# RWKV-7 attention with a SoLU layer on one core: the output product as one run ahead of the transposes

## The chip, the cores and the metric

The program runs on one core of one Trainium2 chip. The metric is the device time of one execution in microseconds, from the runs of the whole kernel; lower is better. Before the change the median of three runs is 536.89 us (536.58, 536.89, 538.34).

## What is computed

Two blocks, all in fp32. First a recurrent attention over 4 batches, 8 heads, 768 positions and head size 40, then a feed-forward layer over the 3072 tokens that come out.

```
for t in range(S):                       # S = 768, state: D x D per batch and head
    y[:, :, t] = rt @ state
    Sa    = state @ at
    state = state * wt - outer(Sa, bt) + outer(vt, kt)

h    = x @ w_in                          # x: 3072 x 320, w_in: 320 x 1024
e    = exp(h - max(h));  solu = h * e / (sum(e) + 1e-9)
ln   = (solu - mean) / sqrt(var + 1e-6) * g_ln
out  = ln @ w_out                        # w_out: 1024 x 320
```

## The kernel before

The recurrence is computed in chunks of 64 positions. A chunk of two batches is one item of work; there are N = 24 items (2 pairs of batches, 12 chunks each), and items alternate between the two pairs of batches, each of which carries its own state. The kernel is a software pipeline written out by hand: every engine runs its instructions in the order in which the program issues them (`manual_schedule`). One turn of the main loop, for i from -1 to 26, is called a slot here. In slot i the kernel works on several items at once:

- item j = i + 5: the transposes of a (`front`) and b (`front_b`), the product of both (`norm`, tile py, result nt), and the start of the inverse of a small triangular matrix. The decay of item j + 2 is summed up (`decay_by_halves`, part of tile pst) and that of j + 1 transposed (`decay_turned`, ei to ex).
- item i + 1: the transposes of k and v (`attend_kv`, tile pkv, copied to kvT), of r (`attend_r`, tile pb, copied to rT) and of the state (`stated`, tile pst, copied to s); the scores (ps), the product of r and the state (psr), then px and the small products in py (`couple`, `close`).
- item i: the solve with the inverse (`solved`, tile pu, masked by VectorE and copied by ScalarE into lu), and the read-out (`read`, tile pyo; `summed` and `leave`, tiles tot, st and x).
- item c = i - 2: the first feed-forward product (`hidden`, tile h), the row maximum (nmax), exponential (e), weighing and spread (sq, var, rs).
- item c - 1: the transposes of e (`folded`, tile plnT, copied to lnT) and the second feed-forward product (`output`, tile po), which ScalarE scales into osb (`stored`) before SP's queue sends it out.

VectorE fills its time with steps of the inverse of two items together: lines 502 to 519, tiles prod and uu. The strings in `plans` say how many steps stand at which place; in slots from 6 on those of the even slots and those of the odd slots differ. In even slots four steps stand between bT and lu, in odd slots one, which is the first of a new inverse. Each step of this size consists of two products and two sums. GpSimd (POOL) scales b and k (line 393, tile kb), takes the power for rs and issues the stores of x and some other DMAs; SP issues most loads and the stores of the output.

PSUM is divided into four pairs of banks: A, B, C and h. A tile gets a pair by its tag, and a new tile with the same tag waits until all readers of the old one are done. From slot 5 on `turn` swaps B and C between the names X and Y in every slot, so that what was X in one slot is Y in the next. In the slots from 5 on, pair A holds in turn the transposes of a and b (pa), the state with the cumulative sums (pst), psr and pyo; X holds pb, ps, px; Y holds pkv, pu, py and po.

A detail that the change touches: from slot 5 to 22 the output product is cut in two (`FIRST = 6`, line 27 and line 1132). Six of its eight blocks of the inner dimension are multiplied at the end of the slot, the other two in the next slot after the transposes of a, b, k and v, followed by the scaling and the store. Each block is two matmuls of 160 columns in the program; the profile shows twice as many, so that a whole product is 32 and the parts are 24 and 8.

The block of the loop that the change edits is the `else` branch of a slot's first half (lines 1011 to 1040). Slot 5 (`i == EARLY - AHEAD`) is the first to run it; there the logarithm of the decay of item 7 (`logged`, tile lw) is issued inside the block. From slot 19 on there are no more items for the transposes of a and b.

Of the kernel before, what the change touches and what calls it, by code (L numbers as in the profile page):

```python
# [21 lines left out]
AHEAD = 5  # L22
LANDS_NEXT = {2: 6, 3: 7, 4: 8, 5: 11, 6: 9, 7: 10, 8: 12}
LAG = 2
EARLY = 10
NK = 5
FIRST = 6
SPLITS = {2: (0, 0, 0, 2, 4), 24: (0, 0, 0, 0, 2)}


# [23 lines left out]
def kernel(  # L54
# [24 lines left out]
    N = NPAIR * NCH  # L79
    NF = DFF // P  # L80
# [64 lines left out]
    def pair(tag, name):  # L145
        return psum.tile([P, 2, 512], FP32, tag=tag, name=name)

    turn = dict(X="B", Y="C")
# [165 lines left out]
    def ok(i):  # L314
        return 0 <= i < N
# [258 lines left out]
    def attend_kv(i, t):  # L574

        if not ok(i):
            return lambda: None
        d = st[i]
        for y, x in enumerate((d["kb"], v_t[0])):
            turned(t, y, x)  # L580
        o = two.tile([P, 2, 8, C], FP32, tag="kvT", name="kvT", bufs=1)
        d["kT"], d["vT"] = o[:, :, 0:4], o[:, :, 4:8]
        return lambda: nc.scalar.copy(out=o[0:W2].rearrange("p b j t -> p b (j t)"), in_=t[0:W2])

    def attend_r(i, t, y):
        if not ok(i):
            return lambda: None
        t = turned(t, y, r_t[0])

        def evict():  # L590
            st[i]["rT"] = kept("rT", t)
        return evict
# [73 lines left out]
    def solved(i):  # L666

        if not ok(i):
            return lambda: None
        d = st[i]  # L670
        t = pair(turn["Y"] if i >= LAG else "h", "pu")
        for u in in_turn(lambda p, q, g, h: (p ^ h, p)):
            p, q, g, h = u
            at, x = (2 * q + g) * W2, half(p ^ h)
            mm(t[half(p), h, at:at + W2], d["tu"][x, 4 * p + 2 * q + g, Q:], x0[x, h, 2 * q + g])
        lu = d["lu"] = two.tile([P, H, W2], FP32, tag="lu", name="lu", bufs=1)
        o, y = lu.rearrange("p (j h) c -> p h j c", h=2), t[:, :, 0:4 * W2].rearrange("p h (j d) -> p h j d", j=4)
        copy = lambda: nc.scalar.copy(out=o[:, :, :, C:], in_=y[:, :, :, C:])
        if i < LAG:
            copy()  # L680
            return lambda: masked(o[:, :, :, 0:C], y[:, :, :, 0:C])
        masked(o[:, :, :, 0:C], y[:, :, :, 0:C])
        return copy
# [159 lines left out]
    late, rest = [], []  # L843
# [129 lines left out]
    for i in range(-1, N + LAG + 1):  # L973
        j, c = i + AHEAD, i - LAG
        plan = plans.get(i, plans[N + i % GRP])
        if len(plan) > 6:
            plan, unflipped = plan[:2] + plan[3:], plan[2]
        else:
            unflipped = ""
        steady = i >= EARLY - AHEAD  # L980
        if i >= 0 and not steady:
            load_keys(j + 3, "w")
        if not steady:
            load_r(i + 3)
        elif i > EARLY - AHEAD and i % GRP:
            load_r(i + 2)
        if i == -1:
            load_values(2)
            land(4, nc.sync)
            land(len(lands), nc.sync)  # L990

        if i < EARLY - AHEAD:
            tc_, ta = pair("C", "pa"), pair("A", "pb")
            front_out, r_out = front(j, ta, 0), attend_r(i + 1, ta, 1)
            fold_out = folded(c - 1)
            ei_out, b_out = decay_turned(j + 1, tc_, 0), front_b(j, tc_, 1)
            kv_out = attend_kv(i + 1, pair(turn["X"], "pkv"))
            r_out()
            front_out()
            if i < EARLY - AHEAD:  # L1000
                vector(plan[0])
                fold_out()
                b_out()
            else:
                b_out()
                vector(plan[0])
                fold_out()
            s_out = stated(i + 1, pair("A", "pst"), 0) if ok(i + 1) else lambda: None
            for evict in (ei_out, kv_out, s_out):
                evict()  # L1010
        else:
            turn.update(zip("XY", ("BC", "CB")[(i - EARLY + AHEAD) % 2]))
            ta = pair("A", "pa")
            front_out, b_out = front(j, ta, 0), front_b(j, ta, 1)
            kv_out = attend_kv(i + 1, pair(turn["Y"], "pkv"))
            front_out()
            kv_out()
            b_out()
            if i == N + LAG:
                fold_out = folded(c - 1)  # L1020
            for products, stored in rest:
                products()
                if i == N + LAG:
                    late.append(stored)
                else:
                    stored()
            rest.clear()
            vector(plan[0])
            if i < N + LAG:
                fold_out = folded(c - 1)  # L1030
            ts = pair("A", "pst")
            s_out = stated(i + 1, ts, 0) if ok(i + 1) else lambda: None
            tc_ = pair(turn["X"], "pb")
            r_out, ei_out = attend_r(i + 1, tc_, 0), decay_turned(j + 1, tc_, 1)
            if i == EARLY - AHEAD and ok(j + 2):
                logged(j + 2)
            cum_out = decay_by_halves(j + 2, ts)
            for evict in (r_out, ei_out, fold_out, s_out, *late):
                evict()
            late.clear()  # L1040
        if not steady:
            left(i - 1)
        if i == EARLY - AHEAD:
            load_keys(j + 3, "w")

        early = i < EARLY - AHEAD or i > N - 2
        waves = (1, 0, 1, 0, 1, 0, 1, 1, 0, 0, 0) if early else (0, 0, 2, 1, 0, 0, 1, 1, 0, 0, 0)
        wave = iter(range(NK))

        def run(x):  # L1050
            for _ in range(waves[x]):
                hidden(c, next(wave))
            if sum(waves[:x + 1]) == NK and sum(waves[:x]) < NK:
                highest(c)

        run(0)
        if i >= EARLY - AHEAD:
            cum_out()
        solved(i)()
        vector(plan[1])  # L1060
        if not steady:
            load_keys(j + 2, "bak")
        run(1)
        scores(i + 1)()
        vector(unflipped)
        flip(i + 1)
        run(2)
        scaled(j + 1, "b")
        stated_r(i + 1)
        run(3)  # L1070
        norm(j)
        if ok(j) and j % GRP == GRP - 1:
            begin_inverse(j // GRP)
        scaled(j + 1, "k")
        by_value(i + 2)
        run(4)
        if i == LAG + 1:
            mean = mean_more(pair("A", "pmean")[:, 0], 6, NF, mean)
        carried(i + 1)
        run(5)  # L1080
        read(i, 0)
        if i >= 0:
            load_values(i + 3)
        if steady:
            left(i - 1)
            load_keys(j + 2, "ba" if i % GRP else "b")
            if i % GRP:
                load_r(i + 3)
        ahead = 2 + (i >= EARLY - AHEAD)
        if ok(j + ahead):  # L1090
            logged(j + ahead)
        vector(plan[2])
        run(6)
        couple(i + 1)()
        if i == LAG + 1:
            centred(mean)
        run(7)
        close(i + 1)
        run(8)
        driven(i + 1)()  # L1100
        run(9)
        read(i, 1)
        run(10)
        exped(c)
        vector(plan[3])
        finish = summed(i)
        vector(plan[4])

        if i < EARLY - AHEAD:
            decay(j + 2, pair("C", "pcum")[:, 0])()  # L1110
        tb = pair(turn["X" if i < EARLY - AHEAD else "Y"], "po")
        weighed(c)
        if i == N - 1:
            finish()
        spreadof(c)
        if i >= 0:
            some(Q, (i + 2) // GRP)
            odd = steady and i % GRP == 1
            if odd:
                load_keys(j + 2, "k")  # L1120
                load_keys(j + 4, "w")
            bring(i + 2)
            if odd:
                load_keys(j + 3, "ak")
                load_keys(j + 5, "w")
        if i != N - 1:
            finish()
        vector(plan[5])
        if i == N + LAG:
            output_last(c - 1)  # L1130
        else:
            output(c - 1, tb[:, 0], NF - 1 if i == N + LAG - 1 else FIRST if EARLY - AHEAD <= i < N - 1 else NF)
        if i == -1:
            turn_g(tb[:, 0])
        if i == LAG - 1:
            mean = mean_more(tb[:, 0], 0, 3)
        if i == LAG:
            mean = mean_more(tb[:, 0], 3, 6, mean)
# [30 lines left out]
```

## Time and profile before

| | value |
|---|---|
| median of 3 runs | 536.89 us |
| span of the profiled execution | 536.5 us |
| mean granted TensorE clock | 0.984 |
| time from the start of one slot's po to the next, slots 12 and 13 | 18.55 and 18.46 us |
| the same, slots 19 to 22 | 17.13, 16.95, 16.96, 16.96 us |
| ScalarE busy | 314.1 us (59%) |

The profile is of one execution. In its timeline a line holds the start of a group of instructions, its length, the engine, the line of the code, what is written from what, the shape, and how many there are; in brackets stands the idle time of the engine before it and what ended it. Matmuls overlap, so a group's end lies a little after the next one's start. PE is the matmul part of TensorE and PEld its weight loads; DVE is VectorE, ACT ScalarE, POOL GpSimd, SP the engine whose queue issues DMAs. The line numbers are those of the kernel before; line 285 is the helper `mm` that records nearly all matmuls, line 400 the helper `turned` of all transposes but those of e (line 804), so tiles tell more than lines.

Slots can be found by the output product: po at the start of slot 5 lies at 163.09 us, of slot 6 at 181.83, of slot 8 at 218.99, of slot 12 at 294.08, of slot 13 at 312.63, of slot 14 at 331.09, of slot 19 at 423.63 and of slot 23 at 491.63. What is counted to a slot here begins with the product that the program issues last in the slot before.

### The profile page before, as it was taken

To read this page: it belongs to the slowest core of one execution; us is meant where nothing else is said; L and a number is where in the kernel's file an instruction comes from. 1 tells how busy PE (TensorE), PEld (TensorE's weight loads), DVE (VectorE), ACT (ScalarE), POOL (GpSimd) and SP (SyncE) were. 2 spreads that over 40 slices of the span, in tenths; PEclk is the share of its full clock that TensorE was granted. 3 is DMA by queue.
4 is the path that set the end of the run, shared out by engine and by line. 5 is a ranking of instruction groups with operands and counts; after the bars stand their busy time and mean duration, and the time that the engine had idled before them with its cause. 6 is when DMAs were issued, how large, how long until landed. Compare 5 with 4: busy or idle time off the path is not lost.

```text
span 536.5 us, 28053 instructions
## 1 busy us (share of the span) xinstructions
PE 480.7 (90%) x12029; PEld 391.0 (73%) x12029; DVE 430.6 (80%) x1752; ACT 314.1 (59%) x627; POOL 227.0 (42%) x376
## 2 busy tenths in 40 slices
PE   4633775798989999999999999999999999999997
PEld 3522665665878878877887887788778877887766
DVE  4599987999997987997998979979989888544322
ACT  3633466488457566556666665666656555654433
POOL 4577538245253344545445263544445331210300
PEclk9999978799999999999999999999999999999999
DMA  8898889765465566674774776675554551421210
GB/s 149 153 157 160 177 142 206 165 134 124 90 131 120 102 125 138 123 151 96 147 156 104 132 150 121 118 155 109 114 118 102 108 111 43 106 65 29 61 53 24
DMA packets 194475, 63.95 MB, mean 119 GB/s; under 512 B 166840, under 2 KB 186528, under 8 KB 194352
## 3 DMA queue, kind: packets, MB, share of 16 engines
q1 hardware_dynamic: 181232, 41.60, 41.8%
q0 software_dynamic: 10768, 19.95, 15.2%
q8 instruction: 94, 1.54, 1.2%
q10 hardware_dynamic: 2352, 0.62, 0.7%
q14 instruction: 29, 0.24, 0.2%
HBM read 47.96 MB, written 14.16 MB: 116 GB/s over the span
## 4 chain that ended last, share of the span: by engine, by line
PE 73%; DVE 17%; DMA 5%; issue 2%; ACT 2%; SPq 0%; POOL 0%; ACTq 0%; POOLq 0%; DVEq 0%
PE po L285 20%; PE h L285 18%; PE px L285 6%; PE pyo L285 5%; PE py L285 5%; DVE prod L516 4%; PE ps L285 4%; DVE uu L519 3%; PE pu L285 3%; PE plnT L804 2%; PE pb L400 2%; PE pa L400 2%; PE psr L285 2%; PE pkv L400 2%; DMA uu_dram<-uu 1%
## 5 line engine op out<-in xcount | busy, mean ns | idle before, releaser
L285 PE MATMUL h<-w_in,xT 64*64 64x512 f32 (+1 forms) x1064 | 121.7, 551 | 0.7 <-issue 0.7
L285 PE MATMUL po<-w,lnT 128*128 128x160 f32 x768 | 115.2, 304 | 0.0
L516 DVE TENSOR_TENSOR prod<-blk,uu 128x48 f32<-128x48 f32 (+19 forms) x576 | 108.1, 227 | 1.3
L285 PEld LDWEIGHTS po<-w,lnT 128*128 128x128 f32 x768 | 105.5, 190 | 4.7 <-issue 0.8
L519 DVE TENSOR_TENSOR uu<-uu,prod 128x48 f32<-128x48 f32 (+19 forms) x576 | 103.8, 219 | 0.0
L483 POOL DMA_DIRECT2D nt_dram<-nt x86 | 50.8, 597 | 84.5 <-ACT nt L475 76.4
L792 POOL TENSOR_TENSOR rs<-var,mhalf 128x1 f32<-128x1 f32 x24 | 17.6, 734 | 138.2 <-ACT var L791 138.1
L761 DVE TENSOR_REDUCE nmax<-h 128x1 f32<-128x1024 f32 x24 | 29.3, 1219 | 32.9 <-PE h L285 32.9
L285 PEld LDWEIGHTS h<-w_in,xT 64*64 64x64 f32 x1064 | 36.7, 133 | 20.4 <-issue 16.7
L790 ACT ACTIVATE sq<-e,mu 128x1024 f32<-128x1024 f32 x24 | 26.9, 1119 | 24.4 <-DVE e L777 24.4
L444 DVE TENSOR_TENSOR lu<-pu,cst 128x512 f32<-128x512 f32 x24 | 16.5, 686 | 26.6 <-PE pu L285 24.8
L769 ACT ACTIVATE e<-h,nmax 128x1024 f32<-128x1024 f32 x24 | 26.7, 1111 | 17.7 <-DVE nmax L761 17.7
L558 ACT ACTIVATE wy<-py,cst 128x256 f32<-128x256 f32 x24 | 11.4, 474 | 39.2 <-PE py L285 37.1
L311 POOL DMA_DIRECT2D raw_r<-in_r_dram x48 | 33.3, 698 | 0.0
L777 DVE SCALAR_TENSOR_TENSOR e<-h,e 128x1024 f32<-128x1024 f32 x24 | 29.2, 1217 | 4.3 <-ACT e L769 4.1
L508 DVE SCALAR_TENSOR_TENSOR uu<-blk,uu 128x30 f32<-128x30 f32 (+3 forms) x144 | 30.2, 262 | 1.7 <-DMA blk<-nt_dram 0.8
L393 POOL TENSOR_TENSOR kb<-raw_b,inv 128x320 f32<-128x320 f32 x24 | 21.4, 894 | 21.1 <-DMA raw_b<-in_b_dram 13.7
L285 PE MATMUL pcum<-lw,cst 128*128 128x160 f32 x48 | 15.1, 461 | 16.7 <-ACT lw L351 16.7
L285 PEld LDWEIGHTS py<-tu,nt 64*64 64x64 f32 x768 | 17.3, 142 | 16.3 <-issue 10.7
L617 ACT COPY st<-psr 128x416 f32<-128x416 f32 (+1 forms) x44 | 14.2, 374 | 24.5 <-PE psr L285 24.4
L664 ACT ACTIVATE x<-px 128x832 f32<-128x832 f32 x24 | 20.7, 864 | 11.0 <-PE px L285 11.0
L710 DVE TENSOR_TENSOR tot<-pyo,st 104x416 f32<-104x416 f32 x44 | 23.8, 581 | 2.9 <-PE pyo L285 2.9
(154 smaller groups left out, 1095.3 us busy)
## 6 DMA issues: line engine op xcount, KB each, us to landing
xT<-x_dram SPq DMA_DIRECT2D x48, 160.0 KB, 4.2
blk<-nt_dram POOLq DMA_DIRECT2D x22, 256.0 KB, 4.7
raw_w<-in_w_dram SPq DMA_DIRECT2D x48, 80.0 KB, 3.3
raw_r<-in_r_dram POOLq DMA_DIRECT2D x48, 80.0 KB, 4.0
lv<-in_v_dram SPq DMA_DIRECT2D x48, 80.0 KB, 3.7
out_dram<-osb SPq DMA_DIRECT2D x46, 80.0 KB, 2.5
a<-in_a_dram SPq DMA_DIRECT2D x44, 80.0 KB, 4.0
raw_k<-in_k_dram SPq DMA_DIRECT2D x42, 80.0 KB, 3.8
```

What stands on the lines that cost most here:

```text
L285: nc.tensor.matmul(o, lhsT=lhsT, rhs=rhs, start=start, stop=stop, skip_group_check=True)
L311: queue.dma_start(out=x[half(p), :, 0:D], in_=ap[2 * bp + p, :, ci * C:(ci + 1) * C, :].rearrange("h t d -> t h d"))
L400: nc.tensor.transpose(out=t[0:W2, p, at + C * j:at + C * j + C], in_=x[half(p), 2 * j:2 * j + 2].rearrange("p a b -> p (a b)")[:, skip:ski ...
L483: queue.dma_start(out=blocks[n][e].rearrange("(a x h) s c -> a x s h c", a=GRP, x=2)[at, x], in_=nt[home:home + Q].rearrange("p h j c -> p ...
L508: nc.vector.scalar_tensor_tensor(out=u[:, c, j + 1:Q], in0=nb[:, j, j + 1:Q], scalar=u[:, c, j:j + 1], in1=u[:, c, j + 1:Q], op0=ALU.mult, ...
L516: nc.vector.tensor_tensor(out=ts[-1], in0=nb[:, j:j + 1, j + 1:Q].to_broadcast([P, hi - lo, m]), in1=u[:, lo:hi, j:j + 1].to_broadcast([P, ...
L519: nc.vector.tensor_tensor(out=u[:, lo:hi, j + 1:Q], in0=u[:, lo:hi, j + 1:Q], in1=x, op=ALU.add)
L710: nc.vector.tensor_tensor(out=by_b(tot)[:, :, :, part], in0=y[:, :, :, part], in1=by_b(state_of(i)[:, x])[:, :, :, 0:HW], op=ALU.add)
L761: nc.vector.tensor_reduce(out=nmax, in_=d["h"], axis=AX.X, op=ALU.max, negate=True)
L769: nc.scalar.activation(out=e, in_=d["h"], func=AF.Exp, bias=d["nmax"], accum_out=d["esum"])
L777: nc.vector.scalar_tensor_tensor(out=d["e"], in0=d["h"], scalar=1.0 / DFF, in1=d["e"], op0=ALU.mult, op1=ALU.mult, accum_out=d["mu"])
L790: nc.scalar.activation(out=pair("A" if i == N - 2 else "h", "sq").rearrange("p a b -> p (a b)"), in_=d["e"], func=AF.Square, scale=-float( ...
```

## The change

Four things change, all from slot 5 on:

1. The output product is no longer cut: all eight blocks are multiplied at the end of the slot, and its scaling and store follow at once. (Slot 25 still leaves one block to slot 26, as before.)
2. The order of the first half of a slot: first the transposes of k and v, then of a and b, then of r and ei, then of e; the transposes of the state and the cumulative sums come last. The copies on ScalarE follow as kvT, rT, ex, lnT, s.
3. The tile of the state and of the cumulative sums (pst) moves from pair A to pair Y, in which pkv has been. The tile of the solve (pu) moves from Y to A, in which the transposes of a and b (pa) have been.
4. ScalarE copies lu before it takes the exponentials of the cumulative sums (`cum_out`), not behind them.

The core of the diff:

```diff
-FIRST = 6
...
-        t = pair(turn["Y"] if i >= LAG else "h", "pu")
+        t = pair("A" if i >= EARLY - AHEAD else turn["Y"] if i >= LAG else "h", "pu")
...
             turn.update(zip("XY", ("BC", "CB")[(i - EARLY + AHEAD) % 2]))
+            kv_out = attend_kv(i + 1, pair(turn["Y"], "pkv"))
             ta = pair("A", "pa")
             front_out, b_out = front(j, ta, 0), front_b(j, ta, 1)
-            kv_out = attend_kv(i + 1, pair(turn["Y"], "pkv"))
+            kv_out()
             front_out()
-            kv_out()
             b_out()
-            if i == N + LAG:
-                fold_out = folded(c - 1)
+            tc_ = pair(turn["X"], "pb")
+            r_out, ei_out = attend_r(i + 1, tc_, 0), decay_turned(j + 1, tc_, 1)
+            fold_out = folded(c - 1)
             for products, stored in rest:
                 products()
-                if i == N + LAG:
-                    late.append(stored)
-                else:
-                    stored()
+                late.append(stored)
             rest.clear()
             vector(plan[0])
-            if i < N + LAG:
-                fold_out = folded(c - 1)
-            ts = pair("A", "pst")
+            r_out()
+            ei_out()
+            fold_out()
+            ts = pair(turn["Y"], "pst")
             s_out = stated(i + 1, ts, 0) if ok(i + 1) else lambda: None
-            tc_ = pair(turn["X"], "pb")
-            r_out, ei_out = attend_r(i + 1, tc_, 0), decay_turned(j + 1, tc_, 1)
             if i == EARLY - AHEAD and ok(j + 2):
                 logged(j + 2)
             cum_out = decay_by_halves(j + 2, ts)
-            for evict in (r_out, ei_out, fold_out, s_out, *late):
-                evict()
+            s_out()
+            for stored in late:
+                stored()
             late.clear()
...
         run(0)
+        solved(i)()
         if i >= EARLY - AHEAD:
             cum_out()
-        solved(i)()
         vector(plan[1])
...
-            output(c - 1, tb[:, 0], NF - 1 if i == N + LAG - 1 else FIRST if EARLY - AHEAD <= i < N - 1 else NF)
+            output(c - 1, tb[:, 0], NF - 1 if i == N + LAG - 1 else NF)
```

## The prediction

> **What bounds the kernel now.** I read the page first. Its first part gives the share of each engine, its chain names PE for 73% of the span.
>
> ```profile
> PE 480.7 (90%) x12029; PEld 391.0 (73%) x12029; DVE 430.6 (80%) x1752; ACT 314.1 (59%) x627; POOL 227.0 (42%) x376
> ```
>
> The table by stretches, cut at the starts of the output product, gives one slot a line (span, then PE, PEld, DVE, ACT, POOL busy, clock, DMA share, GB/s). Slot 12, slot 13, slot 19:
>
> ```profile
> 294.15:312.70 18.55, 18.55 (x510) 15.42 (x509) 16.92 (x77) 11.95 (x25) 7.32 (x13) 1.00 0.71 133
> 312.70:331.16 18.46, 18.46 (x509) 15.32 (x509) 15.67 (x63) 11.92 (x25) 11.19 (x17) 1.00 0.63 132
> 423.70:440.83 17.13, 17.13 (x446) 13.76 (x445) 14.24 (x66) 9.74 (x20) 6.25 (x10) 1.00 0.62 129
> ```
>
> PE has no hole: a slot is the sum of PE's work at a granted clock of 1.00. So what counts is what PE saves and which wait it now meets. The timeline of PE in slot 12 (start, length):
>
> ```profile
> 294.08 3.53 PE L285 MATMUL po<-w,lnT 128*128 128x160 f32 x24
> ...
> 298.26 0.39 PE L400 MATMUL pkv<-cst,v 64*104 64x64 f32 x8
> 298.57 1.35 PE L285 MATMUL po<-w,lnT 128*128 128x160 f32 x8
> 299.86 0.71 PE L804 MATMUL plnT<-cst,e 64*128 64x64 f32 x16
> 300.41 0.39 PE L400 MATMUL pst<-cst,st 64*104 64x64 f32 x8
> 300.63 0.40 PE L400 MATMUL pb<-cst,r 64*104 64x64 f32 x8
> ...
> 305.13 0.65 PE L285 MATMUL psr<-rT,s 40*64 40x64 f32 x32
> ```
>
> All times below are counted from the start of the slot's first po (294.08 here); starts follow one another, since the ends overlap. The reader sees the island: eight po between transposes. Then DVE and POOL in that slot:
>
> ```profile
> 298.24 0.69 DVE L427 TENSOR_TENSOR aT<-pa,ex 104x512 f32<-104x512 f32 x1 [0.38 <-PE pa L400]
> 298.85 0.68 DVE L440 COPY bT<-pa 104x512 f32<-104x512 f32 x1
> ...
> 299.98 1.01 DVE L516 TENSOR_TENSOR prod<-blk,uu 128x60 f32<-128x60 f32 x2
> 300.92 1.01 DVE L519 TENSOR_TENSOR uu<-uu,prod 128x60 f32<-128x60 f32 x2
> ...
> 302.91 0.68 DVE L444 TENSOR_TENSOR lu<-pu,cst 128x512 f32<-128x512 f32 x1
> ```
>
> ```profile
> 300.83 0.88 POOL L393 TENSOR_TENSOR kb<-raw_b,inv 128x320 f32<-128x320 f32 x1
> ```
>
> DVE waits only 0.38 us for the transposes of a and b, then does four steps of the inverse, then lu. Two of the steps' instruction pairs take 1.01 us, where their neighbours take 0.34 to 0.35: DVE is held for 0.67 us twice around POOL's kb, 1.35 us in all. From aT to lu it is 4.67 to 4.73 us in each even slot from 6 to 16. In odd slots only the start of an inverse stands there and DVE then waits 2.24 us for pu.
>
> **What it removes.** Per slot the island goes. From pkv's last group to pst it is now 0.31 + 1.29 + 0.55 us. Without it: 0.23 (a group of eight transposes followed by transposes), 1.09 for eight more po in one run (32 take 4.55 from start to start in slot 23, 24 take 3.46) and 0.50 for plnT (slot 5, which has no island: length 0.66 against 0.71). That saves 0.08 + 0.20 + 0.05 = 0.33 us. Islands lie in slots 6 to 22; slot 23 has its 32 in one run already. In the twelve full slots 6 to 17 that is **-3.96 us**, if nothing waits.
>
> **What it moves, even slots.** New order on PE: po to 4.55, pkv to 5.04, pa to 5.49, pb to 5.94, plnT to 6.44, pst to 6.67, then cumulative sums, pu, ps, 16 h, and psr ready at 11.05 - 0.33 = 10.72. The transposes of a and b end at 5.66, not 4.12, so aT begins at 5.70 instead of 4.16: DVE idles 1.5 us more, though x is done at 3.8 to 4.8. Behind aT nothing has moved on DVE. And pu now lies in pair A, which psr needs next: psr has to wait for lu by DVE and the copy of lu by ACT behind it. From the start of lu: 0.68, 0.04 to ACT (slot 5: lu ends 174.12, copy starts 174.16), 0.43 copy, 0.05 back to PE = 1.20 us. Before, psr waited for neither.
>
> How late lu is hangs on the hold. Three values: none, aT to lu 3.33 (4.67 less 1.35), lu at 9.03, psr free at 10.23, no wait; all 1.35, lu at 10.37, psr at 11.57, **0.85 us** wait. In between: POOL's chain (var, rs, three x_dram, kb) is not moved. In slot 10 rs starts at 4.77, takes 0.56 when DVE leaves it alone, the three DMA issues 1.86, so kb lies at 7.25 to 8.13. DVE's steps start at 5.70 + 1.20 = 6.90; held from there to 7.25 (0.35) and once for 0.67, that is 1.02, lu at 10.05, psr at 11.25, a wait of **0.52 us**. I take this one, as the position of the steps against kb has changed and slot 5 shows it matters (below). Slots 10, 12, 14, 16: 4 x 0.52 = 2.08. Slot 6: lu 0.06 later, 0.58, less some 0.15 that this slot already loses (18.70 for 18.55): 0.43. Slot 8: var ends at 5.68, so osb frees pair X at 6.15 and pb waits 0.66, which covers lu's delay; it loses 0.49 at the same place already: 0.17. **+2.68 us** in all. Odd slots: the start of the inverse ends at 5.70 + 2.25 = 7.95, before pu (8.3): no price.
>
> The Trainium skill, "SBUF — State Buffer", section "Who interferes with whom", says that a DVE instruction with two SBUF inputs contends with a GpSimd instruction that reads SBUF, and one with at most one does not. The page agrees with the two 1.01 us pairs and with aT and bT, which read PSUM, never being stretched; by it those two instructions would now run beside part of POOL's work at no price, and the sum would be -0.65 instead of +1.05 (second rival).
>
> The cover elsewhere: kvT on ACT goes 5.31 to 6.32 (osb first, then 1.01), and pst needs it at 6.44. bT is done at 6.98, pu starts at 7.05. Spare of 0.1 us each; where osb is late both are gone, but psr then waits less by as much. cum_out behind lu's copy is needed a slot later; the out DMA keeps its place in SP's queue, since no other SP issue lies between its old and new place.
>
> **Slot 5.** There the logarithm lw is issued by hand inside this block:
>
> ```profile
> 169.58 0.47 ACT L351 ACTIVATE lw<-raw_w 128x320 f32<-128x320 f32 x1
> ```
>
> It now stands behind rT, ex and lnT on ACT. kvT at 168.27, rT 169.18, ex 169.66, lnT 170.14, lw 171.05 to 171.52: the cumulative sums start at 171.55 instead of 170.47. **+1.08 us**; no island to win there.
>
> **Slots 18 to 23.** Without a and b, pst comes soon and waits for kvT: pkv ends 5.21, kvT 5.25 to 6.26, pst 6.31, pu 6.64; now pu starts at 6.43. The whole saving is lost and 0.21 more: 4 x 0.21 = 0.84 in slots 19 to 22. Slot 18 has a and b, and pu there waits for bT until 7.02 against 6.88: 0.14. Slot 23 puts plnT into pair A, so pu waits for lnT's copy (496.93 to 497.95) until 498.00 instead of 497.73: 0.27. Together **+1.25 us**.
>
> **Sum.** -3.96 + 2.68 + 1.08 + 1.25 = +1.05 us on the profiled span of 536.5. The median of the runs is 536.89, 0.4 above; forecast **538.0 us**. Some 0.3% (1.6 us) is what a measurement tells from no change, so this is no change, leaning to slower.
>
> **Rivals.**
> 1. *Aligned hold (slower).* POOL waits its turn and DVE is held both times in full, as in all six even slots now: waits of 0.85 x 4, 0.91 - 0.15 and 0.88 - 0.49, together 4.55 instead of 2.68: +2.9, 539.8 us. If moreover the later lu pushes tot, osb and pb in the following odd slots by the same 0.52 (six times 3.1), 543. It decides from a lu later than 9.52, in even slots, at psr. For it: the 4.67 to 4.73 are very steady. Against: the kb now falls mostly under aT and bT.
> 2. *One hold.* The steps meet kb only once, as slot 5 has it, whose kb lies at 169.25 and whose first instruction of the inverse is the only one clearly stretched:
>
> ```profile
> 169.43 1.26 DVE L502 TENSOR_TENSOR uu<-blk,above 64x512 f32<-64x512 f32 x1
> ```
>
> Its nominal length is 0.67, so +0.59. With 0.67, lu at 9.70, psr waits 0.18: 4 x 0.18, 0.24 - 0.15, 0.17, together 0.98: -0.65, 536.3 us (0.65 less than 536.89, rounded). The rule of the Trainium skill's page quoted above leads here.
> 3. *The waits stay away (faster).* kvT and lu are in time and the islands of slots 18 to 22 pay too: -17 x 0.33 + 1.08 + 0.27 = -4.3, 532.6 us. With only psr's wait gone, -1.6: 535.3. For it: DVE idles some 3.8 us in slots 12 and 13 together (0.38 before aT, 0.96 before nmax, then 0.23 before aT, 2.25 before lu), so it has time to catch up. Against: it idles before aT and cannot work ahead there.
>
> **How the numbers follow.** The forecast 0.40 (0.27 of it no change, 0.13 slower), the aligned hold 0.28 (slower), one hold 0.14 (0.06 no change, 0.08 faster), no waits 0.18 (faster). Faster 0.26, same 0.33, slower 0.41. The range goes from 533.5, most of the third rival, to 543.0, the first with its follow-up; the forecast alone would be 536.5 to 539.7.
>
> **What would show it.** One po group of 32 per slot (4.55 us) and plnT directly behind pb: the gain. aT with some 1.9 us of idle time behind pa in every slot, psr with a wait for ACT lu of about 0.5 us in even slots only. pst waiting for kvT in slots 19 to 22. In slot 5 a wait of about a microsecond for lw. A psr that waits in odd slots too, or no wait at psr at all, proves the sum wrong. Slots 12 and 13, 37.01 us together now, should take 36.9; 36.4 would say that nothing waits, 37.2 that the hold is whole.

## The result and the profile after

The kernel after takes 542.65 us (median of four runs, 540.68 to 543.30) where the kernel before took 536.74 beside it (535.64 to 538.34): a ratio of 1.0099, 95% interval 1.0071 to 1.0128. It is slower by about 1%, outside what a measurement of this kernel mistakes for no change. The forecast was 538.0.

The profiled execution of the kernel after is its fastest, 540.68 us with a span of 538.6. The first lines of its page, engines and then DMA queues (packets, MB, share of 16 engines):

```profile
PE 480.0 (89%) x12029; PEld 397.6 (74%) x12029; DVE 428.2 (80%) x1752; ACT 315.4 (59%) x627; POOL 224.6 (42%) x376
...
q8 instruction: 94, 1.54, 1.2%
```

PE's busy time fell by 0.7 us and PE is still the bound, so the time came as holes. They are not where the mean would show them: the code ahead of slot 5 is the same in both kernels, but it took 160.75 us in this execution and 163.09 in that of before (in the profiles of this study, from 160.8 to 167.7). So the two are compared from the start of slot 5 to that of slot 23: 328.5 us before, 332.6 after, **+4.1 us**. The spans of the two profiled executions differ by 2.1 us only (the head 2.3 shorter, the tail 0.4 longer), the medians by 5.9; what makes the rest of that, no profile shows. Slots 12, 13 and 19 of after by stretches:

```profile
293.29:312.58 19.29, 18.74 (x513) 16.32 (x509) 16.49 (x80) 12.00 (x25) 7.71 (x13) 1.00 0.69 137
312.58:330.72 18.14, 18.14 (x510) 15.57 (x508) 16.00 (x61) 11.95 (x25) 11.19 (x17) 1.00 0.61 125
424.14:441.31 17.17, 17.00 (x449) 13.58 (x445) 14.42 (x67) 9.86 (x20) 6.42 (x10) 1.00 0.58 124
```

Slot 13 is 0.32 us shorter than before, as an island is worth; slot 12 is 0.74 longer, and PE is idle in it for 0.55 us. The timeline of PE in slot 12 (start, length, and in brackets the idle time ahead with what ended it):

```profile
293.29 4.61 PE L284 MATMUL po<-w,lnT 128*128 128x160 f32 x32
...
299.22 0.66 PE L803 MATMUL plnT<-cst,e 64*128 64x64 f32 x16
299.72 0.39 PE L399 MATMUL pst<-cst,st 64*104 64x64 f32 x8
...
301.28 0.69 PE L284 MATMUL ps<-aT,kvT 40*64 40x64 f32 x30
301.81 0.28 PE L284 MATMUL ps<-rT,kvT 40*64 40x64 f32 x2
302.55 0.63 PE L284 MATMUL ps<-rT,kvT 40*64 40x64 f32 x27 [0.47 <-issue]
...
304.69 0.68 PE L284 MATMUL psr<-rT,s 40*64 40x64 f32 x29
```

po is one run of 32 and plnT follows pb, as the change says. But psr, which the prediction let wait, has no bracket, and a hole stands in the middle of ps, two matmuls after its second half began: the same operands, the same tile, no data to wait for. The profile calls the releaser "issue". DVE and POOL in the same slot:

```profile
298.98 0.69 DVE L426 TENSOR_TENSOR aT<-pa,ex 104x512 f32<-104x512 f32 x1 [1.89 <-PE pa L399]
...
300.45 1.02 DVE L518 TENSOR_TENSOR uu<-uu,prod 128x64 f32<-128x64 f32 x2
...
301.66 0.34 DVE L518 TENSOR_TENSOR uu<-uu,prod 128x60 f32<-128x60 f32 x2
...
302.98 0.68 DVE L443 TENSOR_TENSOR lu<-pu,cst 128x512 f32<-128x512 f32 x1
```

```profile
300.06 1.19 POOL L392 TENSOR_TENSOR kb<-raw_b,inv 128x320 f32<-128x320 f32 x1
```

aT has its 1.89 us of idle time and begins 5.69 us into the slot (forecast 1.9 and 5.70). DVE is held around kb once, for 0.68 us, not twice: lu begins 9.69 us into the slot.

**What "issue" is here.** The page of the profile counts 12,029 matmuls and as many weight loads, 24,058 instructions, and 94 packets of 16 KB on the queue called instruction: 256 instructions a packet, so this is read as PE's program, which arrives while it runs. The test of this reading is the place of the holes. The trace has 177 semaphore and drain instructions of PE besides; counted with these, each hole of over 0.05 us that is put down to "issue" between slots 5 and 23 begins at place 193 or 194 of a page of 256, in the kernel before (2 holes), in that after (12) and in every other kernel below that has such holes. For slot 12, from the records of PE and of that queue, the three borders at which a slot's small matmuls lie:

```
          border reached  next page's fetch   PE goes on   after landing
before    302.91          298.95 to 299.88    302.94       3.06
          307.01          303.86 to 304.93    307.01       2.08
          310.75          308.09 to 309.54    310.78       1.24
after     301.87          299.32 to 301.17    302.55       1.38
          306.68          304.38 to 305.30    306.69       1.39
          310.47          308.14 to 309.45    310.77       1.32
```

The fetch of the next page begins when PE is some way into the present one (0.7 us at the first border before, 0.9 after), takes 0.88 to 1.85 us (median 1.03 before, 1.00 after), and where PE stood still its first new instruction came 1.22 to 1.60 us after the landing. The page that ends in ps held the island: from border to border PE had work for 4.65 us (298.26 to 302.91). Without the island it has 3.49 (298.38 to 301.87), and the fetch with its lead needs 0.94 + 1.85 + 1.38 = 4.17. With a fetch of the median length it would have needed 3.32, and PE would not have stood still here. The landing of the long one, by the DMA view cut to 299.2 to 301.3 us (5.5% of 16 engines in 2.1 us is 1.85 us of one packet):

```profile
q8 instruction: 1, 0.02, 5.5%
```

From slot 5 to 23 the kernel before stands still for over 0.15 us, from one start to the next, at 2 of 70 borders, 1.38 us together; the kernel after at 14, 6.21 us. The difference of 4.8 us is more than the loss of 4.1. The fetches are no longer than before. The page that ends in ps has become shorter: in slots 6 to 17 PE has work for 4.67 us in it before and 3.37 after (means of 12), and 4 of the 12 now end in a stall, 1.8 us together. The other stalls of after, 9 at px and py and one in psr, 4.4 us, end pages that lost no island (px 4.01 us before, 4.21 after; py 3.75 and 3.73); there the fetch began later in the page (1.70 us for 1.09 in px, 1.43 for 1.24 in py), and no run shows why.

### The profile page after: what moved, and what is told of

The parts are those of the page before. It is cut to its first block, busy times and chain, and to the rows that moved or that the text cites. A ratio compares the mean times of both kernels' runs of the same rounds, so it can differ in the third digit from the quotient of the medians.

```text
span 538.6 us, 28053 instructions
## 1 busy us (share of the span) xinstructions
PE 480.0 (89%) x12029; PEld 397.6 (74%) x12029; DVE 428.2 (80%) x1752; ACT 315.4 (59%) x627; POOL 224.6 (42%) x376
## 4 chain that ended last, share of the span: by engine, by line
PE 67%; DVE 20%; DMA 5%; ACT 4%; issue 3%; POOL 0%; SPq 0%; ACTq 0%; POOLq 0%; DVEq 0%
PE po L284 19%; PE h L284 16%; PE px L284 5%; PE py L284 5%; PE pyo L284 5%; DVE prod L515 5%; DVE uu L518 4%; PE ps L284 4%; PE pu L284 3%; DVE uu L507 2%; PE psr L284 2%; DMA uu_dram<-uu 1%; PE plnT L803 1%; PE pkv L399 1%; PE pst L284 1%
## 5 line engine op out<-in xcount | busy, mean ns | idle before, releaser
L284 PE MATMUL h<-w_in,xT 64*64 64x512 f32 (+1 forms) x1064 | 124.7, 551 | 1.0 <-issue 1.0
L284 PE MATMUL po<-w,lnT 128*128 128x160 f32 x768 | 110.7, 302 | 0.0
L515 DVE TENSOR_TENSOR prod<-blk,uu 128x48 f32<-128x48 f32 (+19 forms) x576 | 104.6, 221 | 1.3
L791 POOL TENSOR_TENSOR rs<-var,mhalf 128x1 f32<-128x1 f32 x24 | 13.8, 576 | 139.5 <-ACT var L790 139.5
L284 PEld LDWEIGHTS h<-w_in,xT 64*64 64x64 f32 x1064 | 41.3, 133 | 19.0 <-issue 15.3
L426 DVE TENSOR_TENSOR aT<-pa,ex 104x512 f32<-104x512 f32 x18 | 12.4, 691 | 30.2 <-PE pa L399 26.8
L507 DVE SCALAR_TENSOR_TENSOR uu<-blk,uu 128x30 f32<-128x30 f32 (+3 forms) x144 | 32.7, 279 | 1.6 <-DMA blk<-nt_dram 0.8
L392 POOL TENSOR_TENSOR kb<-raw_b,inv 128x320 f32<-128x320 f32 x24 | 22.6, 941 | 21.2 <-DMA raw_b<-in_b_dram 13.8
L284 PEld LDWEIGHTS py<-tu,nt 64*64 64x64 f32 x768 | 18.7, 142 | 13.8 <-issue 7.5
```

Of the source, the lines that this page charges most:

```text
L284: nc.tensor.matmul(o, lhsT=lhsT, rhs=rhs, start=start, stop=stop, skip_group_check=True)
L392: nc.gpsimd.tensor_tensor(out=kb[:, j:j + H, 0:D], in0=d["raw_" + n], in1=heads(d["inv"]), op=ALU.mult)
L507: nc.vector.scalar_tensor_tensor(out=u[:, c, j + 1:Q], in0=nb[:, j, j + 1:Q], scalar=u[:, c, j:j + 1], in1=u[:, c, j + 1:Q], op0=ALU.mult, ...
L515: nc.vector.tensor_tensor(out=ts[-1], in0=nb[:, j:j + 1, j + 1:Q].to_broadcast([P, hi - lo, m]), in1=u[:, lo:hi, j:j + 1].to_broadcast([P, ...
```

## The experiments

Theory F: PE waits for pages of its own program. Its rivals are the waits of the prediction: W (psr waits for lu in even slots), L (lw in slot 5), K (pst waits for kvT in slots 19 to 22). A page cannot be made longer alone, but its border can be moved: idle matmuls at the very start push all later instructions on, and change no order, buffer or wait behind them; the head gets longer where there are many. In all kernels with them, line numbers are 6 higher.

### fill8: the borders 32 instructions earlier

```diff
     nc.vector.memset(mhalf, -0.5)
+    still = const.tile([C, C], FP32, name="still")
+    nc.vector.memset(still, 0.0)
...
+    idle = pair("B", "idle")
+    for _ in range(8):
+        nc.tensor.matmul(idle[0:C, 0, 0:8], lhsT=still, rhs=still[:, 0:8], start=True, stop=True, skip_group_check=True)
```

> The kernel after with 8 idle matmuls (64x64 by 64x8 on zeros) put ahead of PE's first work, in the 6.7 us in which PE waits for its first data. Each is 4 instructions in PE's stream, so every later instruction of PE lies 32 places further on and the borders of the 256-instruction pages fall 32 places earlier in the code; no wait on data, no order and no buffer changes. Theory F (the loss comes from PE waiting for the next page of its own instructions): in the profile of after, the sum over slots 5 to 23 of what the pages fall short of the time a fetch needs goes from 9.4 to 5.6 by my estimate from its own PE records, so 2 to 4 us faster than after: 538.5 to 540.5. Theories W (psr waits for lu, 2.7 us in all), L (lw in slot 5, 1.1) and K (pst waits for kvT in slots 19 to 22, 0.8): none of these waits hangs on where a page ends, so as after, within 0.5 us.

540.14 us, ratio 1.0039 (1.0020 to 1.0059), 0.6% below the ratio of after. Slots 5 to 23 take 328.8 us, 3.8 less than in after: F's upper end. Steps of over 0.15 us at borders are left in 3 places, 0.77 us together, and PE is idle for "issue" nowhere in these slots. In their stead a wait has come up; slot 10 in the timeline of PE:

```profile
265.54 0.64 PE L290 MATMUL ps<-aT,kvT 40*64 40x64 f32 x28
...
268.83 0.69 PE L290 MATMUL psr<-rT,s 40*64 40x64 f32 x32 [0.42 <-ACT lu L683]
```

ps runs through, and now psr waits for lu, in slots 6, 8, 10, 12, 14 and 16 by 0.49, 0.29, 0.42, 0.16, 0.32 and 0.35 us. The odd slots 7, 9, 11, 13 and 15 take 18.10 to 18.15 us, 0.32 to 0.36 less than before: the island's gain, whole.

### fill48 and fill32: 192 and 128 instructions earlier

Only the number changes (48, 32).

> As fill8 with 48 idle matmuls: 192 places, so the page borders fall 192 places earlier in the code, which puts one of the four borders of a slot just behind the run of small matmuls and transposes. Theory F: by the same estimate the sum of what pages fall short rises from 9.4 to some 30 us: 10 to 25 us slower than after, 553 to 568. Theories W, L and K: as after, within 0.5 us.

550.07 us, ratio 1.0208 (1.0179 to 1.0236). The total lies 3 us below F's range, and not for F's reason alone: slots 5 to 23 take 335.1 us, 2.5 more than after, a quarter of the least expected. The rest is the head: 48 idle matmuls took 10.4 us, so PE's first real work began at 11.34 us, not at 6.67.

```profile
1.01 10.40 PE L161 MATMUL idle<-still 64*64 64x8 f32 x96 [1.01 <-DVE still L106]
...
310.62 1.51 PE L290 MATMUL h<-w_in,xT 64*64 64x512 f32 x12 [0.46 <-issue]
```

The second line shows what matters: the stalls have left ps and py, and this one stands in front of h, 192 places earlier in the code, at the moved border. My estimate of the size, made from how long pages last, was far too coarse.

> As fill8 with 32 idle matmuls, 128 places. Theory F: by what the places of 0, 32 and 192 gave in slots 5 to 23 (332.6, 328.8 and 335.2 us), and with an estimate of 19 us for what the pages fall short (9.4 at 0, 5.6 at 32, 30 at 192): between 332 and 336 us, with the stalls at other instructions than in after; the head some 2 us longer, as the idle matmuls took 0.108 us each pair in fill48. W: 332.6 as after.

554.83 us, ratio 1.0312 (1.0281 to 1.0344); slots 5 to 23 take 341.1 us, 8.5 more than after and 5 above F's range. No instruction of these slots differs from after's. The steps of over 0.15 us at borders are 17.6 us in 27 places, of which 11 (3.8 us) show no idle time of PE: most lie where h ends, and PE takes steps of 0.2 to 0.4 us there without a border too (0.41 from h to py in each slot of the kernel before). The idle time that is left, 9.3 us, lies almost all in pyo and psr:

```profile
279.69 0.49 PE L290 MATMUL pyo<-lu,kb 64*64 64x104 f32 x10 [1.11 <-issue]
...
339.32 0.57 PE L290 MATMUL pyo<-lu,kb 64*64 64x104 f32 x12 [1.05 <-issue]
...
370.26 0.40 PE L290 MATMUL psr<-rT,s 40*64 40x64 f32 x12 [0.47 <-issue]
378.44 0.57 PE L290 MATMUL pyo<-lu,kb 64*64 64x104 f32 x12 [1.08 <-issue]
```

The queue called instruction has 95 packets here, as in fill8: the added instructions begin a new one.

### before_fill8 and before_fill32: the same shift in the kernel before

> The kernel before with the same 8 idle matmuls (32 places). Theory F: before has stalls of this kind too, 1.4 us seen from slot 6 on; at this place the estimate falls from 10.4 to 5.0, so what can be won is at most those 1.4 us and some in the head: 0 to 2 us faster than before. W, L, K: as before, within 0.5 us.

540.54 us, ratio 1.0040 (1.0014 to 1.0066): a miss, since nothing should have become slower. The profile does not show the loss: slots 5 to 23 take 329.1 us (328.5 before), the steps of over 0.15 us at borders 1.59 us, 0.11 of it idle time. Its runs spread from 537.3 to 544.7; where the excess lies is open.

> The kernel before with 32 idle matmuls, 128 places, as fill32. Theory F in its general form (where a page ends decides, in either kernel; the change of order only moved one such place): in the kernel after this shift cost 8.5 us in slots 5 to 23 (332.6 to 341.1); the same small runs of matmuls stand around the same borders in the kernel before, so 5 to 12 us longer in that stretch, 334 to 341 us instead of 328.5, with waits of 0.5 to 1.2 us at pyo and psr that nothing but the page explains. Rival (only the order of the kernel after has pages that run out): 328.5 within 1 us in slots 5 to 23, the whole at most 2 us longer by the idle matmuls.

543.12 us, ratio 1.0113 (1.0080 to 1.0146); slots 5 to 23 take 334.2 us, 5.7 more, F's lower end. Of the 22 steps of over 0.15 us at borders, 11.2 us together, only nine are stalls, 6.4 us, all in the same pyo; the others are h's own step of some 0.4 us, without idle time of PE:

```profile
352.22 0.58 PE L291 MATMUL pyo<-lu,kb 64*64 64x104 f32 x14 [1.18 <-issue]
```

So the kernel before is not safe from this; its borders lay well. With the borders at the same 32 places, after against before is 328.8 to 329.1 us in slots 5 to 23: with its stalls out of the way the change gains next to nothing, as the waits of the prediction take the islands' gain.

### steps_late and fill8_steps: psr's wait taken away, at both places of the borders

```diff
-        24: ("o2 2", "", "", "o9", "o4", "", ""),
+        24: ("", "o2 2", "", "o9", "o4", "", ""),
```

> The kernel after with the four steps of the inverse that stand ahead of lu on DVE in even slots put behind lu (same instructions, same place for all other engines). Theory W (the prediction's: psr waits in six even slots for lu, 2.68 us in all): 2.0 to 2.7 us faster than after. Theory F: psr's own wait is only 0.67 us in slot 6 and 0.2 elsewhere; no instruction of PE moves, so 0.9 us faster at most, and the stalls at page borders stay where they are.

542.83 us, ratio 1.0079 (1.0057 to 1.0102); slots 5 to 23 take 332.4 us against 332.6. W's 2.0 to 2.7 us did not come; the stalls are 5.84 us at 15 borders, much as in after. lu is early now and PE waits for the page all the same, at the end of slot 6 for instance:

```profile
200.38 0.36 PE L284 MATMUL py<-uh,wy 64*64 64x32 f32 x10 [0.64 <-issue]
```

> fill8 and steps_late together: 8 idle matmuls ahead, and the four steps of the inverse behind lu in even slots. In the profile of fill8, whose slots 6 to 22 show no wait for a page of instructions above 0.1 us, psr waits for ACT's copy of lu by 0.49, 0.29, 0.42, 0.16, 0.32 and 0.35 us in slots 6, 8, 10, 12, 14 and 16: 2.03 us. Theory FW (the prediction's wait was there, but hidden in after behind stalls at page borders that took the same time): 1.5 to 2.0 us faster than fill8, about 538.3. Theory F alone (psr's waits are nothing that costs time): as fill8, within 0.5 us; steps_late on the other place of the borders won 0.2 us in slots 5 to 23.

538.37 us, ratio 1.0009 (0.9992 to 1.0026), 0.3% (1.6 us) below fill8's, as FW expects, though the two intervals overlap a little. By the profile slots 5 to 18 take 240.6 us against fill8's 242.0 and no psr waits; slots 18 to 23 take 1.7 us more, 1.0 of it in slot 19 (18.49 for 17.45 us), where 0.76 us pass at one border; over the whole stretch the profile so shows no gain (329.2 for 328.8). The same edit is worth 0.4 us in slots 5 to 18 where the pages run out and 1.4 where they do not: the two waits hid each other.

### lw_pst: slot 5 and the late slots

```diff
             vector(plan[0])
+            if i == EARLY - AHEAD and ok(j + 2):
+                logged(j + 2)
             r_out()
...
-            ts = pair(turn["Y"], "pst")
+            ts = pair(turn["Y"] if ok(j) else "A", "pst")
...
-        t = pair("A" if i >= EARLY - AHEAD else turn["Y"] if i >= LAG else "h", "pu")
+        t = pair("A" if EARLY - AHEAD <= i < N - AHEAD else turn["Y"] if i >= LAG else "h", "pu")
```

> The kernel after with two edits for the waits that the prediction names outside the full slots: in slot 5 the logarithm lw is put on ACT right behind kvT and ahead of rT, and from slot 19 on pst goes into pair A and pu into pair Y again, as in the kernel before. Theory L and K (each of these waits costs its full length): slot 5 about 1.1 us shorter (19.87 to 18.8), slots 19 to 22 about 0.2 each (17.17 to 16.96), slot 23 0.3 (12.10 to 11.79): together 2.2 us faster than after. Rival (other work, kvT or a page border, is next in line at once): less than 1 us.

538.62 us, ratio 1.0025 (1.0006 to 1.0044), more than forecast; slots 5 to 23 take 329.2 us, 3.4 less than after. Slots 20 to 23 take 16.86, 16.87, 16.87 and 11.78 us (after: 17.17, 17.70, 17.17, 12.10), 0.09 to 0.10 below the kernel before (slot 23: 0.01): K is right, and some 0.1 of the island's 0.33 us comes besides. Slot 19 stayed at 17.14. Slot 5 won half of what L said, 19.87 to 19.33 us, since psr was next in line:

```profile
173.37 0.69 PE L284 MATMUL psr<-rT,s 40*64 40x64 f32 x32 [1.10 <-ACT lu L677]
```

The other 1.4 us, in slots 6 to 18, are about what this execution had less of stalls at borders (4.78 us for 6.21).

### Towards a kernel that beats both

> All edits together on the kernel after: 8 idle matmuls, steps behind lu, lw ahead of rT, pst in A from slot 19 on. If the four causes add up: fill8 (slots 5 to 23 in 328.8 us) less 2.0 (psr), 1.1 (lw), 0.8 (pst) and 0.3 (slot 23): about 324.6 us for slots 5 to 23, against 328.5 of the kernel before; 4 us faster than before in that stretch, a ratio of 0.992 to 0.994. If they stand in for one another: 327 to 329, a ratio of 0.998 to 1.003.

538.03 us, ratio 1.0007 (0.9986 to 1.0028); slots 5 to 23 take 328.2 us. Slots 5 to 18 add up (240.0 us, 5.2 less than after: 3.2 of fill8, 1.4 of the steps, 0.5 of lw), but 18 to 23 take 88.3, with 18.81 in slot 19. I put that down to the steps behind lu. In slot 5 psr waited 0.79 us for lu. So the next two leave the steps where they were from slot 18 on, and take some of slot 5's behind lu:

```diff
-        5: ("7", "", "7", "2", "1", "o1"),
+        5: ("4", "3", "7", "2", "1", "o1"),
+        **{n: ("o2 2", "", "", "o9", "o4", "", "") for n in (18, 20, 22)},
```

> fill8_all with two plans of the inverse mended: in slots 18, 20 and 22 the steps stand ahead of lu again (behind it, slots 19 to 21 took 18.81, 17.21 and 17.46 us instead of 17.45, 17.17 and 17.16), and in slot 5 three of the seven steps go behind lu (psr waited 0.79 us for lu there). From fill8_all's 328.2 us in slots 5 to 23: 2.4 less for slots 18 to 23 (88.3 to 85.9), 0.5 to 0.8 less for slot 5, so 325.2 us against 328.5 before: about 3 us faster than the kernel before, a ratio of 0.993 to 0.997. Rival (a page border or osb is next in line): 327 to 328.5, a ratio of 0.998 to 1.001.

536.98 us, ratio 0.9989 (0.9966 to 1.0013); slots 5 to 23 take 328.1 us: the rival. Slot 19 still takes 19.00 with the steps of slots 18 and 20 back in place, 1.12 of it at one border, so the steps were not the cause there. A border and osb are next in line:

```profile
296.77 0.43 PE L405 MATMUL pb<-cst,r 64*104 64x64 f32 x8 [0.40 <-ACT osb L864]
...
437.85 0.39 PE L290 MATMUL pyo<-lu,kb 64*64 64x104 f32 x2 [0.87 <-issue]
```

> best8 with 12 idle matmuls instead of 8, so 48 places instead of 32: the borders fall 16 instructions earlier than in best8. Theory F: the estimate of what pages fall short is nearly flat between these places (5.6 and 5.8 us against 9.4 at 0), so the stretch from slot 5 to 23 within 1.5 us of best8's. If it differs by more, the estimate is too coarse to place a border by.

536.88 us, ratio 0.9992 (0.9971 to 1.0012); 327.4 us, within the 1.5 us of best8. What is left is pb, which waits for osb to empty pair X:

```profile
411.02 0.43 PE L405 MATMUL pb<-cst,r 64*104 64x64 f32 x8 [1.01 <-ACT osb L864]
```

The last kernel puts the fold's transposes ahead of pb:

```diff
+            fold_out = folded(c - 1)
             tc_ = pair(turn["X"], "pb")
             r_out, ei_out = attend_r(i + 1, tc_, 0), decay_turned(j + 1, tc_, 1)
-            fold_out = folded(c - 1)
```

> best12 with the transposes of the layer's result (plnT, pair h) ahead of those of r and the decay (pb, pair X) on PE. In best12 the full slots show one wait left: pb waits for ACT's osb, which empties pair X, by 0.92, 0.27, 0.23, 0.26, 0.23, 0.24 and 1.01 us in slots 6, 8, 10, 12, 14, 16 and 18: 3.16 us; plnT waits for nothing of that kind and takes 0.50 us of PE. If osb is the last cause: 0.5 + 5 x 0.25 + 0.5 = 2.2 us less in slots 5 to 23 (327.4 to 325.2), a ratio of 0.994 to 0.997 to the kernel before. Rival (rT, which ACT copies out of pb, is now late for ps by the same time): within 0.7 us of best12.

536.40 us beside 537.84 of the kernel before, ratio **0.9974** (0.9956 to 0.9992): just faster than before, and 1.3% below the ratio of after. Slots 5 to 23 take 323.9 us, 4.6 less than before and 3.5 less than best12, more than the 2.2 expected; 0.7 of it lies in slot 21, where best12 stood at a border, and the ratio ends just above its range. Most of these 4.6 do not reach the whole: in the two kernels with 12 idle matmuls slot 5 began at 164.2 and 165.9 us, later than in the eleven profiles with 0, 8 or 32 (160.8 to 163.4). Whether the head's own borders do that, and whether 8 would keep more, was not tried.

All of them by the same count, from slot 5 to slot 23: borders with a step of over 0.15 us from one start to the next, their sum, and the idle time of PE that the profile puts down to "issue", all of it at borders (worked out from the trace's records):

```
kernel          slots 5-23   borders   sum us   idle us   ratio to before
before             328.5        2       1.38     0.94     1
after              332.6       14       6.21     3.03     1.0099
fill8              328.8        3       0.77     0        1.0039
fill32             341.1       27      17.62     9.34     1.0312
fill48             335.1       24      10.92     2.32     1.0208
before_fill8       329.1        4       1.59     0.11     1.0040
before_fill32      334.2       22      11.24     4.20     1.0113
steps_late         332.4       15       5.84     2.51     1.0079
fill8_steps        329.2        3       1.82     0.51     1.0009
lw_pst             329.2       13       4.78     2.20     1.0025
fill8_all          328.2        5       2.49     1.18     1.0007
best8              328.1        4       2.44     1.15     0.9989
best12             327.4       11       3.21     0.44     0.9992
best12_fold        323.9       13       2.76     0        0.9974
```

The two counts bound the stalls. The sum is too high where a border lies in or behind h, whose matmuls start 0.2 to 0.4 us apart anyway (fill32, fill48, before_fill32, best12 and best12_fold: none of the 13 of best12_fold is a stall that the profile shows); the idle time is too low, since a matmul's end is modelled, and in fill8_steps 0.44 us at a border are put down to a DMA. Both exceed the time lost where a stall only stands in for another wait. One execution each, so a microsecond between two rows says little.

## Why the prediction was right and wrong

The side it leaned to was right and the time lay in its range, but 538.0 was 4.7 us low, and the working would not have led to 542.65. That the range reached so far is luck: its upper end, 543.0, belongs to a rival whose cause did not occur.

**Where it failed.** "PE has no hole: a slot is the sum of PE's work", and from it "-3.96 us, if nothing waits". The waits were then looked for among tiles and engines, and PE's own program was not among them, though the profile of before had the signs: a queue called instruction, and two holes put down to "issue" in slots 8 and 14:

```profile
236.78 0.37 PE L285 MATMUL py<-uh,wy 64*64 64x32 f32 x12 [0.29 <-issue]
348.69 0.37 PE L285 MATMUL py<-uh,wy 64*64 64x32 f32 x12 [0.65 <-issue]
```

The islands' 0.33 us are real (odd slots of fill8, 0.32 to 0.36), but an island also kept a page of PE's program long enough for the next to arrive. The new order cost 4.8 us of stalls: 1.8 at the pages that held the islands, the rest at others, whose link to the change is not shown. Neither the forecast nor any of the rivals has that cause.

The Trainium skill, "Runtime: NRT & Kernel Launch", section "Instruction fetch mechanics", says that an engine's program comes in blocks of 16 KiB, 256 instructions, the next fetched while the present one runs, and that this is mostly hidden. The trace agrees with the blocks (94 packets for 24,058 instructions) and, for the kernel before, with "mostly": 2 of 70 borders. For the others it does not: 14 of 70 in after, and 16 of 69 with idle time in fill32.

**Right in mechanism, hidden in effect: psr (+2.68).** The start of aT (5.69), its idle time and the chain from lu to psr came as worked out. In after itself PE is idle at psr only in slot 6 (0.47 us); in slots 10, 12 and 16 it had stood at the border in ps just ahead of it (0.41, 0.68 and 0.41 us), in slots 8 and 14 for 0.1 there; with the borders moved the wait appears in all six even slots, 2.03 us in all. It was mis-sized by 0.65: slot 12 met the hold once, as the second rival has it (lu at 9.70, measured 9.69), and slot 10 of fill8 for 1.3 us. The Trainium skill, "SBUF — State Buffer", section "Who interferes with whom", named in the prediction, has a DVE instruction with two SBUF inputs contend with GpSimd, and one with at most one not, outside DVE's two-port modes; the trace agrees, aT and bT beside POOL's work took 0.68 to 0.69 us.

**Right: slot 5 (+1.08).** It grew by 1.13 us, the cumulative sums start 8.46 us into the slot for 7.38 before, and the wait is where it was said to be:

```profile
169.21 0.62 PE L284 MATMUL pst<-lw,cst 64*64 64x160 f32 x5 [1.75 <-ACT lw L350]
```

lw_pst shows the limit of such a term: with lw early, lu is late next, and half of it stays.

**Right, somewhat small: slots 18 to 23 (+1.25).** Slots 19 to 22 lost 0.04, 0.22, 0.74 and 0.21 us (0.21 each was forecast; 0.53 of slot 21 is a page), slot 23 0.31 (0.27). Slot 18 lost 0.50 for 0.14, as pb waited 0.49 us for osb there. In slot 19 of after, ACT and then PE:

```profile
429.38 1.01 ACT L582 COPY kvT<-pkv 104x1024 f32<-104x1024 f32 x1
```

```profile
430.45 0.43 PE L399 MATMUL pst<-cst,st 64*104 64x64 f32 x8
```

pst starts 0.06 us after kvT ends, 6.31 us into the slot, as forecast.

**The rivals.** The aligned hold named about the right time (539.8 to 543) for a wrong reason: in slot 12 DVE was held once instead of twice, and slot 13, which follows it, is 0.32 us shorter, not longer. Slots 12 and 13, "37.2 if the hold is whole", took 37.43, of which 0.98 are two stalls at borders; this sign alone would have confirmed a false cause. The sign that points the right way is the one at psr: about 0.5 us was to be seen in the even slots, and five of the six show no idle time there. The rival without waits is not borne out either: with the stalls gone, in fill8, the waits for lu, lw and kvT are all there.

## What to carry to other kernels

Where an engine with a long unrolled program is the bound, ask of each edit what it does to the time that 256 of its instructions last; a run of long instructions among short ones may be what covers the next page's arrival, and taking it out can then cost more than it saves. Before an order is judged by 1%, move its borders by a few idle instructions at the start: the same order differed by 12 us (fill8 to fill32). A wait that is taken away without gain may have been covered by another, so try it again with that one gone.

## What was not expected of the hardware

- PE stops at the border of a 256-instruction page when it reaches it earlier than about 1.4 us (1.22 to 1.60 in after) after the fetch of the next has landed. A fetch took 0.88 to 1.85 us in before and after. In after it began from 0.5 us before PE reached the page ahead of it to 2.4 after (in fill8 from 1.7 before). What starts a fetch, and what fills the 1.4 us, no run here shows; the estimate from page lengths missed slots 5 to 23 by 7 us and more in fill48 and by 5 in fill32.
- Where POOL's kb meets DVE's steps, DVE is held by about 0.67 us for an instruction: once in slot 12 of after (a pair in 1.02 us), twice in slot 10 of fill8 (1.67), where free pairs take 0.34 to 0.35. kb itself took 1.19 us in slot 12 of after, where DVE was held once, and 0.88 in slot 10 of fill8 and in slot 12 of the kernel before, where it was held twice.
- A matmul of 64 by 64 with 8 columns on an idle PE took 0.108 us each for 96 in a row into one place (fill48), seven times the 0.015 us of ps's 64 with 64 columns in slot 5 of the kernel before (0.95 us from the first start to the last); why was not tried.
